# Splitting attention rows into 16-bit planes on two engines instead of one, in a top-k attention and ELU kernel

## Chip, cores and metric

The kernel runs on one core of a Trainium2 chip. The metric is the device time of one execution in microseconds (us). An engine of the core is named as the profile names it: PE is TensorE (PEld its weight loads), DVE is VectorE, ACT is ScalarE, POOL is GpSimd, SP is SyncE, which here only issues DMAs. Each engine works through its own instructions in the order in which the program lists them, and waits on semaphores for the others.

## The reference

Attention over 8 batches, 8 heads, 576 positions and 64 dimensions, in which each query keeps only its 32 highest scores; then a feed-forward layer with an ELU over all 4608 tokens.

```python
scores = q @ k.T / sqrt(64)                     # (8, 8, 576, 576)
kth    = np.partition(scores, -32)[..., -32]    # the 32nd highest of each row
scores = np.where(scores >= kth, scores, -1e9)
attn   = exp(scores - rowmax); attn /= attn.sum() + 1e-9
x      = (attn @ v), heads side by side         # (4608, 512)
h      = x @ w_in                               # (4608, 2048)
g      = np.where(h > 0, h, np.exp(np.minimum(h, 0)) - 1)
out    = g @ w_out                              # (4608, 512)
```

In the kernel the weight matrices arrive as words of 64 bits and are decoded on the chip in the first steps.

## The kernel before, in words

The attention is cut into 144 **steps**. A step is one tile of 128 queries (or the 64 left over of two heads) for two heads: a score tile `sc` of 128 partitions by 2 rows of 576 numbers (here "row 0" and "row 1": one head each). Work on one step is spread over several rounds of the main loop (lines 839 to 885). Round n does, in program order:

- the transfers and transpositions of keys, queries and values planned for this round (lines 840, 841; `load_halves` issues eight DMAs on SP, `load_v` four);
- the scores of step n+2: PE matmuls (L338), and ACT copies them to `sc` (L346);
- `attend` for a group whose transposed weights are expected (L489 on PE, L516 on ACT);
- `spread` for step n-1: a small subtraction on POOL (L379) from which the exponential of the mask takes its bias;
- `select` for step n: DVE finds the 32 highest in four passes of MAX8 and MATCH_REPLACE8 (L358, L365, L372), listed between the other things as quarters of the round;
- `mask` for step n-1, row 0 after the first quarter, row 1 after the second: two ACT passes over a row (L399, L400), the second an exponential with its sum;
- the transposition of the attention weights of step n-2, called `done`. Up to round 12 PE turns them in nine blocks of 128 by 128 (`turn`, L435) and ACT copies them out (L436). From round 13 on a path over memory is used: `split` copies a row of `sc` on ACT into two planes of 16-bit halves (L451) and SP writes the planes to a buffer in DRAM, `halves` (L452); after row 1, `cross` reads the buffer with a transposing DMA into `et` (L461);
- `normalise` for step n-1 at the end of the round: five small POOL operations (L410 to L414), then a scaling of each row (L416).

After each quarter `feed` places pieces of the feed-forward layer that are due: `hidden` (PE matmuls L564; ACT L574, L577, L579, L583), the ELU sums ("gates", POOL L534), and `project` or `product` (PE L592, L654; ACT L662; POOL L610). The pieces are chosen when the program is written, from costs and due times, so the order on each engine is fixed. `product` also streams prepared weight tiles `tw` through SP (L696).

What the order of the work around the change hangs on:

- the tile `planes` has one buffer (`late["p"]`, `bufs=1`, line 218): a second split waits until the DMA of the first has landed;
- `halves` has three buffers, `et` two, `sc` five;
- SP issues in program order: a transfer that waits for its data holds back all behind it;
- `turned` notes the round of the `cross` with the group, and the main loop calls `attend` in the second round after that (lines 847, 848).

In round n of the kernel before, row 0 of step n-2 is split at the start of the round, row 1 after the second quarter, and the transposing DMA is issued after the third. In the last two rounds the two steps left are split as well.

Of the kernel before, what the change touches and what calls it, by code (L numbers as in the profile page):

```python
# [24 lines left out]
class Tile:  # L25
# [6 lines left out]
    def __init__(self, b, qt, rows, block, cols):  # L32
        self.b, self.qt, self.rem = b, qt, qt == 4
        self.rows = rows
        self.block = block
        self.cols = cols
        self.ql = cols.stop - cols.start
# [21 lines left out]
class Step:  # L59
# [7 lines left out]
    def __init__(self, t, hp, group, at):  # L67
        self.t, self.hp = t, hp
        self.group, self.at = group, at
        self.masked = self.normal = self.turned = False  # L70
        if t.rem:
            rows = [(4 * hp, 0), (4 * hp + 2, 0), (4 * hp + 3, 1), (4 * hp + 1, 1)]
            self.heads = [
                (h, i, slice(64 * (n % 2), 64 * (n % 2) + 64))
                for n, (h, i) in enumerate(rows)
            ]
        else:
            self.heads = [(2 * hp + i, i, slice(0, 128)) for i in range(2)]
# [3 lines left out]
def kernel(  # L82
# [9 lines left out]
    nc = tc.nc  # L92
# [115 lines left out]
    def settle():  # L208

        if decode or late or blocks[0].left or any(x[3] == 0 for x in ffn):  # L210
            return
        raws.close()
        late["f"] = ctx.enter_context(tc.tile_pool(name="f", bufs=2))
        late["g"] = ctx.enter_context(tc.tile_pool(name="g", bufs=2))
        late["x"] = ctx.enter_context(tc.tile_pool(name="xt", bufs=2))
        late["e"] = ctx.enter_context(tc.tile_pool(name="e", bufs=2))
        late["t"] = ctx.enter_context(tc.tile_pool(name="t", bufs=TB))
        late["p"] = ctx.enter_context(tc.tile_pool(name="p", bufs=1))
        late["in"] = ctx.enter_context(tc.tile_pool(name="in", bufs=2))
# [100 lines left out]
    def turn_qk(whole=False):  # L320
        while turning:
            if next(turning[0], turning) is turning:
                turning.pop(0)
            elif not whole:
                return
# [25 lines left out]
    def select(u, more=False):  # L351

        u.first = small.tile([P, 2, 8], FP32, tag="m1", name="m1")
        u.last = small.tile([P, 2, 8], FP32, tag="m4", name="m4")
        cur = [u.sc[:, i, :] for i in range(2)]
        found = [u.first[:, i, :] for i in range(2)]
        for i in range(2):
            nc.vector.max(found[i], cur[i])  # L358
        if more:
            hook()  # L360
        yield
        wk = [wkpool.tile([P, S], FP32, tag=f"wk{i}", name="wk")[:] for i in range(2)]
        for r in range(TOP_K // 8 - 1):
            for i in range(2):
                nc.vector.match_replace(wk[i], found[i], cur[i], TAKEN)  # L365
            cur = wk
            for i in range(2):
                if r < TOP_K // 8 - 2:
                    found[i] = small.tile([P, 8], FP32, tag=f"m{i}", name="m")[:]
                else:  # L370
                    found[i] = u.last[:, i, :]
                nc.vector.max(found[i], cur[i])  # L372
            hook()
            yield

    def spread(u):

        u.den = small.tile([P, 8], FP32, tag="den", name="den")
        nc.gpsimd.tensor_tensor(  # L379
            u.den[:, 2:4], u.last[:, :, 7], u.first[:, :, 0], ALU.subtract  # L380
        )
# [22 lines left out]
    def normalise(u):  # L404

        if u.normal:
            return
        u.normal = True
        den, rec = u.den[:, 4:6], u.den[:, 6:8]
        nc.gpsimd.tensor_scalar_add(den, u.den[:, 0:2], EPS)  # L410
        nc.gpsimd.tensor_tensor(rec, den, power[:], ALU.pow)
        nc.gpsimd.tensor_tensor(den, den, rec, ALU.mult)
        nc.gpsimd.tensor_scalar(den, den, -1.0, 2.0, ALU.mult, ALU.add)
        nc.gpsimd.tensor_tensor(rec, rec, den, ALU.mult)  # L414
        for i in range(2):
            nc.gpsimd.tensor_scalar(  # L416
                u.sc[:, i, :], u.sc[:, i, :], rec[:, i : i + 1], 1.0, ALU.mult, ALU.mult
            )
# [23 lines left out]

    def split(u, i):

        if u.turned:
            return
        if i == 0:
            u.halves = halves.tile([P, 2, 2, S], U16, tag="h", name="halves")
        t = late["p"].tile([P, 2, S], U16, tag="p", name="planes")
        words = u.sc[:, i, :].bitcast(U16).rearrange("p (k w) -> p w k", w=2)  # L450
        nc.scalar.copy(t[:], words)  # L451
        nc.sync.dma_start(u.halves[:, :, i, :], t[:])  # L452

    def cross(u):

        if u.turned:
            return
        g = u.group
        if g.et is None:
            g.et = etpool.tile([P, 2 * J + 1, len(g.tiles), P], FP32, tag="et", name="et")  # L460
        nc.sync.dma_start_transpose(  # L461
            g.et[:, :, u.at, :].bitcast(U16),
            u.halves[:].rearrange("q w i k -> (q w) (i k)"),
        )
        turned(u)

    def turned(u):

        u.turned = True
        if u.at == len(u.group.tiles) - 1:  # L470
            closing.append((place[0] // 4, u.group))

    def attend(g):
        t = g.tiles[0]
# [47 lines left out]
    place = [0]  # L522

    def close_gates(keep=0, upto=None):

        while gates:
            put, group, dst, n, apart = gates[0]
            if put > place[0] - keep if upto is None else group > upto:  # L530
                return
            gates.pop(0)
            if apart:
                nc.gpsimd.tensor_tensor(dst, n, dst, ALU.add)  # L534
                continue
            nc.vector.scalar_tensor_tensor(
                out=dst, in0=n, scalar=-1.0, in1=dst, op0=ALU.add, op1=ALU.add
            )
# [190 lines left out]
    while ends:  # L729
        n = 1 if len(blocks) <= J or len(ends) <= J + 1 else 2  # L730
# [5 lines left out]
    for b in range(B):  # L736
        first[b] = len(steps)
        tiles = []
        for qt in range(J + 1):
# [8 lines left out]
            t = Tile(b, qt, rows, blk, slice(c0, c0 + n))  # L748
# [3 lines left out]
        for qts in orders[b]:  # L752
# [3 lines left out]
            for qt in qts:  # L756
                n = len(steps)
                tiles[qt].block.ready = n + 2.0 if n <= tight else n + 3.25
    NS = len(steps)
# [37 lines left out]
    def feed(n, share):  # L797

        place[0] += 1
        close_gates(2 if n > tight + 3 else 6)  # L800
        fed["at"] = max(fed["at"], n)
        ahead = [(w - fed["sum"]) / (x - fed["at"]) for x, w in due if x > fed["at"]]
        if ahead:
            fed["over"] += max(0.0, share * min(ahead))
        fed["at"] += share
        while ffn and decoded[0] >= ffn[0][1] and 0.5 * ffn[0][0] <= fed["over"]:
            cost, _, piece, _ = ffn.pop(0)
            fed["over"] -= cost
            fed["sum"] += cost
            piece()  # L810
            settle()
# [22 lines left out]
    def step(n):  # L834
        return steps[n] if 0 <= n < NS else None

    closing, settled = [], tight + 4
    main, rest, other = slice(0, J), slice(J, J + 1), slice(J + 1, 2 * J + 1)
    for n in range(NS + 3):
        for fn, args in todo.pop(n, []):  # L840
            fn(*args)
        ahead, cur, prev, done = step(n + 2), step(n), step(n - 1), step(n - 2)
        passes = select(cur, n < tight) if cur else iter(range(4))
        if ahead and n > 1:
            scores(ahead)
        steady = settled <= n < NS
        while steady and closing and closing[0][0] < n - 1:
            attend(closing.pop(0)[1])
        if prev and n > tight:
            spread(prev)  # L850
        crossed = n > settled
        if done and crossed:
            split(done, 0)
        next(passes)
        feed(n, 0.25)
        while closing and not steady:
            attend(closing.pop(0)[1])
        if prev:
            mask(prev, 0, n <= tight)
        if n > 1:  # L860
            turn_qk()
        next(passes)
        feed(n, 0.25)
        if done and not crossed:
            turn(done, main)
            turn(done, rest)
        elif done:
            split(done, 1)
        if prev:
            mask(prev, 1, n <= tight)  # L870
        next(passes)
        feed(n, 0.25)
        if done and not crossed:
            turn(done, other)
        elif done:
            cross(done)
        next(passes)
        if prev:
            normalise(prev)
        if spare and n >= first[1] - 2:  # L880
            difference(*spare.pop(0))
        feed(n, 0.25)
        turn_qk(True)
        if n < 2:
            scores(ahead)
# [36 lines left out]
```

## Time and profile before

| | |
|---|---|
| median of three executions | 1848.02 us (1846.99 to 1848.38) |
| the profiled execution | 1837.74 us, of which the span of the instructions is 1835.6 us |
| mean granted TensorE clock | 0.919 |
| instructions | 26765 |
| POOL busy, DMA moved | 875.2 us, 271.92 MB |

The span runs from the first to the last instruction of the program; the profile gives for each engine the time in which it executes ("busy"), and for each idle time what ended it: `A <- B` means that A waited and that B released it. The timeline lists instructions with start, duration, engine and line; neighbours of one kind are merged with their count. The chain of waits goes back from the last instruction to whatever released it, and again from there.

### The profile page before, as it was taken

The numbers are of one execution on the slowest core, as the hardware profiler recorded it, in microseconds if no ns is written. First come the engines' busy times: TensorE is split into PE (matmuls) and PEld (weight loads), VectorE is DVE, ScalarE is ACT, GpSimd is POOL, SyncE is SP. The second block draws the span as 40 slices with busy tenths as digits, with TensorE's granted clock in tenths as the row PEclk, the third lists the DMA queues.
The fourth block names the chain that finished last, engine by engine and source line by source line (L and its number), as shares of the span: only waits on it lengthen the run. The fifth ranks groups of instructions, "written<-read, shape, count | busy, mean of one in ns | idle before, by whom it ended". The sixth has DMA issues, their size and how long they took to land.

```text
span 1835.6 us, 26765 instructions
## 1 busy us (share of the span) xinstructions
PE 1496.8 (82%) x8535; PEld 1109.2 (60%) x8535; DVE 1460.6 (80%) x2976; ACT 1316.5 (72%) x2321; POOL 875.2 (48%) x1535
## 2 busy tenths in 40 slices
PE   4798878777888787987888696977888787889988
PEld 3476645545666566765666575755666565667765
DVE  6999998777888697978787399887878769788900
ACT  6977757658695767786778677785859576768861
POOL 4963335434554454545454536353544535363430
PEclk9799998888998998998999898998899889899999
DMA  7503544564748575667657665748564665564440
GB/s 231 190 24 75 132 131 133 137 161 117 213 117 215 128 194 136 175 156 167 174 156 174 154 169 125 206 110 217 124 183 128 171 159 156 156 165 116 116 112 22
DMA packets 603340, 271.92 MB, mean 148 GB/s; under 512 B 496704, under 2 KB 565824, under 8 KB 603200
## 3 DMA queue, kind: packets, MB, share of 16 engines
q1 hardware_dynamic: 602000, 269.92, 56.3%
q8 instruction: 68, 1.11, 0.3%
q14 instruction: 72, 0.59, 0.1%
q10 hardware_dynamic: 1200, 0.30, 0.1%
HBM read 99.61 MB, written 92.08 MB: 104 GB/s over the span
## 4 chain that ended last, share of the span: by engine, by line
ACT 26%; PE 22%; DMA 18%; DVE 11%; POOL 10%; SPq 7%; issue 6%; DVEq 0%; ACTq 0%; POOLq 0%
DMA halves<-planes 14%; ACT planes L451 8%; PE ops L654 8%; PE hps L564 5%; DVE wk L365 5%; ACT sc L399 4%; ACT sc L400 4%; PE ops L592 4%; DVE m L372 3%; PE avps L489 3%; DMA tw<-kept 3%; POOL sc L416 2%; SPq L238 2%; PE scps L338 2%; ACT sc L346 2%
## 5 line engine op out<-in xcount | busy, mean ns | idle before, releaser
L564 PE MATMUL hps<-xT,w_in 128*128 128x256 f32 (+1 forms) x2944 | 574.1, 354 | 96.1 <-ACT gT L577 91.7
L372 DVE MAX8 m<-wk 128x8 f32<-128x576 f32 x864 | 609.6, 745 | 7.4 <-POOL den L379 7.2
L564 PEld LDWEIGHTS hps<-xT,w_in 128*128 128x128 f32 x2944 | 487.6, 203 | 179.2 <-ACT gT L577 104.0
L451 ACT COPY planes<-sc 128x1152 uint16<-128x1152 uint16 x266 | 306.8, 1153 | 308.7 <-DMA halves<-planes 245.1
L365 DVE MATCH_REPLACE8 wk<-m,wk 128x576 f32<-128x576 f32 x576 | 422.9, 741 | 0.0
L358 DVE MAX8 m<-sc 128x8 f32<-128x576 f32 x288 | 203.3, 747 | 222.4 <-ACT sc L346 221.0
L410 POOL TENSOR_SCALAR den<-den 128x2 f32<-128x2 f32 x144 | 32.3, 225 | 719.6 <-ACT sc L400 718.5
L654 PE MATMUL ops<-tw,gT 128*128 128x256 f32 x832 | 219.2, 419 | 97.1 <-DMA tw<-kept 79.2
L654 PEld LDWEIGHTS ops<-tw,gT 128*128 128x128 f32 x832 | 167.1, 207 | 141.2 <-DMA tw<-kept 89.1
L400 ACT ACTIVATE sc<-sc,den 128x576 f32<-128x576 f32 x288 | 223.3, 775 | 36.2 <-POOL den L379 20.2
L489 PE MATMUL avps<-et,vT 128*64 128x128 f32 (+2 forms) x2400 | 199.3, 316 | 53.5 <-DMA et<-halves 48.9
L338 PE MATMUL scps<-kqT 64*128 64x288 f32 (+1 forms) x1280 | 205.5, 458 | 30.9 <-ACT kqT L314 12.6
L399 ACT ACTIVATE sc<-sc,m 128x576 f32<-128x576 f32 x288 | 223.2, 775 | 0.4 <-DVE m L372 0.4
L416 POOL TENSOR_SCALAR sc<-sc,den 128x576 f32<-128x576 f32 x288 | 213.5, 751 | 14.9
L489 PEld LDWEIGHTS avps<-et,vT 128*64 128x64 f32 x2400 | 138.8, 145 | 124.6 <-issue 52.9
L365 DVE MATCH_REPLACE8 wk<-m,sc 128x576 f32<-128x576 f32 x288 | 211.4, 741 | 0.0
L654 PE MATMUL ops<-w_out,gT 128*128 128x256 f32 x624 | 160.6, 413 | 45.2 <-POOL den L410 23.9
L534 POOL TENSOR_TENSOR gT<-n,gT 128x512 f32<-128x512 f32 x136 | 173.3, 1275 | 41.6 <-ACT n L583 41.5
L346 ACT ACTIVATE sc<-scps 128x576 f32<-128x576 f32 x288 | 169.9, 642 | 28.8 <-PE scps L338 28.6
L338 PEld LDWEIGHTS scps<-kqT 64*128 64x128 f32 (+1 forms) x1280 | 110.9, 191 | 107.7 <-issue 32.9
L654 PEld LDWEIGHTS ops<-w_out,gT 128*128 128x128 f32 x624 | 125.5, 207 | 78.8 <-POOL den L410 26.7
L592 PE MATMUL ops<-w_out,gT 128*128 128x512 f32 x320 | 145.1, 606 | 0.7 <-POOL tw L711 0.7
(57 smaller groups left out, 1257.8 us busy)
## 6 DMA issues: line engine op xcount, KB each, us to landing
halves<-planes SPq DMA_DIRECT2D x266, 288.0 KB, 2.6
tw<-kept SPq DMA_DIRECT2D x208, 256.0 KB, 3.8
raw<-in_moe_w_in_dram SPq DMA_DIRECT2D x16, 512.0 KB, 5.0
vT<-in_v_dram SPq DMA_DIRECT2D x64, 128.0 KB, 2.7
raw<-in_moe_w_out_dram SPq DMA_DIRECT2D x16, 512.0 KB, 3.8
out_dram<-osb SPq DMA_DIRECT2D x32, 256.0 KB, 4.3
kin<-in_k_dram SPq DMA_DIRECT2D x112, 72.0 KB, 2.8
qin<-in_q_dram SPq DMA_DIRECT2D x112, 72.0 KB, 2.7
```

Of the source, the lines that this page charges most:

```text
L338: nc.tensor.matmul(wide[i][rows, half, 0:HS], kq[part, q0 : q0 + u.t.ql], kq[part, k0 : k0 + HS], start=True, stop=True,)
L346: nc.scalar.activation(u.sc[:, i, :].rearrange("p (a s) -> p a s", a=2), wide[i][:, :, 0:HS], AF.Copy, scale=scale,)
L365: nc.vector.match_replace(wk[i], found[i], cur[i], TAKEN)
L372: nc.vector.max(found[i], cur[i])
L399: nc.scalar.activation(sc, sc, AF.Prelu, scale=-1.0, bias=low, alpha=1.0 / STEEP)
L400: nc.scalar.activation(sc, sc, AF.Exp, scale=-STEEP, bias=gap, accum_out=u.den[:, i : i + 1])
L416: nc.gpsimd.tensor_scalar(u.sc[:, i, :], u.sc[:, i, :], rec[:, i : i + 1], 1.0, ALU.mult, ALU.mult)
L451: nc.scalar.copy(t[:], words)
L489: nc.tensor.matmul(ps[i * D : (i + 1) * D, cols], vt[:, 2 * J + i if c == J else i * J + c, :], w, start=(c == 0), stop=(c == J),)
L564: nc.tensor.matmul(blk.h[:, f % bank, :], w_in[:, i, f * P : (f + 1) * P], blk.xT[:, i, 0:n_tok], start=(i == 0), stop=(i == NC - 1),)
L592: nc.tensor.matmul(blk.o[:], blk.gT[f // NG][:, f % NG, s * P : (s + 1) * P], w_out[:, f, :], start=(f == 0), stop=(f == NF - 1),)
L654: nc.tensor.matmul(sums, x[:, f, :], w, start=opens and f == 0, stop=f == NG - 1, skip_group_check=not opens,)
```

## The change

A step's row 1 is split on POOL, at the end of the round in which the step was normalised (round n-1 for step n-2), with the same shapes and the same `planes` buffer. Its write to DRAM is kept as a function and issued in the next round after the second quarter. Row 0 is split on ACT as before, but after the third quarter, half a round later than before. The transposing DMA is moved from after the third quarter of round n to after the first quarter of round n+1 (`past` is step n-3 seen from there), and the number noted for its group is reduced by one, so that `attend` comes in the same round as before. The last two steps (rounds 144 and 145) go back to `turn` on PE.

```diff
     def split(u, i):
 
-        if u.turned:
-            return
-        if i == 0:
+        if u.halves is None:
             u.halves = halves.tile([P, 2, 2, S], U16, tag="h", name="halves")
         t = late["p"].tile([P, 2, S], U16, tag="p", name="planes")
         words = u.sc[:, i, :].bitcast(U16).rearrange("p (k w) -> p w k", w=2)
-        nc.scalar.copy(t[:], words)
-        nc.sync.dma_start(u.halves[:, :, i, :], t[:])
+        if i == 0:
+            nc.scalar.copy(t[:], words)
+        else:
+            nc.gpsimd.tensor_copy(t[:], words)
+        return lambda: nc.sync.dma_start(u.halves[:, :, i, :], t[:])
...
         if u.at == len(u.group.tiles) - 1:
-            closing.append((place[0] // 4, u.group))
+            closing.append((place[0] // 4 - (u.halves is not None), u.group))
...
-        crossed = n > settled
-        if done and crossed:
-            split(done, 0)
+        crossed = settled < n < NS
+        past = step(n - 3)
         next(passes)
+        if past and past.halves is not None:
+            cross(past)
         feed(n, 0.25)
...
         elif done:
-            split(done, 1)
+            done.write()
         if prev:
             mask(prev, 1, n <= tight)
         next(passes)
...
         elif done:
-            cross(done)
+            split(done, 0)()
         next(passes)
         if prev:
             normalise(prev)
+            if settled <= n < NS - 1:
+                prev.write = split(prev, 1)
```

`Step` gets two new fields, `halves` and `write`, both empty at first.

More of the change, by code (lines that the diff above doesn't have):

```diff
@@ L70, in __init__ @@
         self.masked = self.normal = self.turned = False
+        self.halves = self.write = None
         if t.rem:
@@ L450, in split @@
         words = u.sc[:, i, :].bitcast(U16).rearrange("p (k w) -> p w k", w=2)
-        nc.scalar.copy(t[:], words)
-        nc.sync.dma_start(u.halves[:, :, i, :], t[:])
+        if i == 0:
[3 more added lines that the diff above has]
+        return lambda: nc.sync.dma_start(u.halves[:, :, i, :], t[:])
     def cross(u):
-        if u.turned:
-            return
         g = u.group
```

## Prediction

> **What bounds the kernel now.** I read the busy times and the chain of waits on the page first, then the waits of ACT, then two steps of the timeline.
>
> ```profile
> span 1835.6 us, 26765 instructions
> ...
> PE 1496.8 (82%) x8535; PEld 1109.2 (60%) x8535; DVE 1460.6 (80%) x2976; ACT 1316.5 (72%) x2321; POOL 875.2 (48%) x1535
> ...
> DMA halves<-planes 14%; ACT planes L451 8%; PE ops L654 8%; PE hps L564 5%; DVE wk L365 5%; ACT sc L399 4%; ACT sc L400 4%; PE ops L592 4%; DVE m L372 3%; PE avps L489 3%; DMA tw<-kept 3%; POOL sc L416 2%; SPq L238 2%; PE scps L338 2%; ACT sc L346 2%
> ```
>
> By busy time PE and DVE lead. But 22% of the chain are the ACT copies into the planes and the writes of the planes. The waits say why:
>
> ```profile
> ACT planes L451 <- DMA halves<-planes: 245.1, 93, 8.0
> ACT planes L451 <- POOL sc L416: 62.4, 45, 2.7
> ACT e L662 <- PE ops L654: 41.1, 23, 5.7
> ACT sc L346 <- PE scps L338: 28.6, 24, 2.4
> ACT osb L662 <- PE ops L654: 25.9, 16, 2.5
> ...
> ACT xT L516 <- PE avps L489: 21.1, 13, 3.8
> ACT sc L400 <- POOL den L379: 20.2, 20, 2.4
> ACT n L574 <- PE hps L564: 13.2, 8, 3.0
> ...
> DVE m L358 <- ACT sc L346: 221.0, 79, 11.9
> PE avps L489 <- DMA et<-halves: 48.9, 29, 4.0
> ```
>
> ACT is busy for 1316.5 us and waits 307.5 us before the splits and some 150 us in the other rows shown: nearly the whole span is spoken for. ACT has no slack, while DVE waits for ACT (221 us). So ACT's order, with what it waits for, sets the pace.
>
> ```profile
> 1000.04 1.15 ACT L451 COPY planes<-sc 128x1152 uint16<-128x1152 uint16 x1 [2.95 <-DMA halves<-planes]
> 1001.10 0.77 ACT L399 ACTIVATE sc<-sc,m 128x576 f32<-128x576 f32 x1
> ...
> 1001.90 0.77 ACT L400 ACTIVATE sc<-sc,den 128x576 f32<-128x576 f32 x1
> 1002.59 0.19 ACT L400 ACTIVATION_READ_ACCUMULATOR sc<-sc,den 128x1 f32 x1
> 1002.68 0.57 ACT L574 ACTIVATE n<-hps 128x512 f32<-128x512 f32 x1
> ...
> 1003.79 3.68 PE L564 MATMUL hps<-xT,w_in 128*128 128x256 f32 x8 [3.98 <-ACT gT L577]
> 1003.80 2.12 SPq L461 DMA_TRANSPOSE et<-halves  x1
> ...
> 1004.29 0.63 ACT L583 ACTIVATE n<-n 128x512 f32<-128x512 f32 x1
> ...
> 1005.88 1.15 ACT L451 COPY planes<-sc 128x1152 uint16<-128x1152 uint16 x1
> 1006.02 2.28 SPq L238 DMA_DIRECT2D kin<-in_k_dram  x4
> ...
> 1008.40 2.17 SPq L238 DMA_DIRECT2D qin<-in_q_dram  x4
> ...
> 1010.66 4.62 SPq L452 DMA_DIRECT2D halves<-planes  x2
> ...
> 1011.03 5.45 PE L564 MATMUL hps<-xT,w_in 128*128 128x256 f32 x24
> ...
> 1013.56 1.15 ACT L451 COPY planes<-sc 128x1152 uint16<-128x1152 uint16 x1 [2.74 <-DMA halves<-planes]
> ```
>
> The split at 1005.88 ends at 1007.0, but SP is busy with eight key and query loads until 1010.6; only then does it issue the write, and the next split waits for the landing, until 1013.56. From the start of a split to the landing of its write are 3.76 us where SP is free (1000.04 to 1003.80, where the transposing DMA, which waits for it, is issued).
>
> ```profile
> L451 ACT COPY planes<-sc x266: 1134/1152/1184, 163.8 to 1783.9; 128x1152 uint16<-128x1152 uint16 x133
> L452 SPq DMA_DIRECT2D halves<-planes x266: 533/553/1033, 171.6 to 1785.1; - x133
> DMA to landing us min/median/max: 2.5/2.6/5.9
> ```
>
> These 266 splits are 133 rounds in 1621 us (163.8 to 1785.0): 12.2 us a round. The change touches this stretch and the end. The busy times in it (160 to 1780), of its last part with granted clock, DMA share and GB/s at the end of the row, and summed over six parts:
>
> ```profile
> 1560.00:1780.00 220.00, 202.49 (x1399) 154.85 (x1400) 151.47 (x311) 170.27 (x298) 100.59 (x189) 0.95 0.50 134
> sum 1620.00, PE 1326.64 PEld 989.96 DVE 1314.63 ACT 1175.09 POOL 768.68; mean PE 221.11 PEld 164.99 DVE 219.10 ACT 195.85 POOL 128.11
> ```
>
> ACT is busy 8.9 us a round here, PE 10.0, DVE 9.9.
>
> **Part by part.** *ACT loses* 133 copies of 1.152 us, 153 us, and the waits before them, 307.5 us. The copy that stays waits for other things, and the wait before the exponential grows, as follows.
>
> *POOL gains* 133 copies of 128x1152 16-bit numbers, a kind that the trace does not show there. The nearest rows:
>
> ```profile
> L416 POOL TENSOR_SCALAR sc<-sc,den 128x576 f32<-128x576 f32 x288 | 213.5, 751 | 14.9
> L534 POOL TENSOR_TENSOR gT<-n,gT 128x512 f32<-128x512 f32 x136 | 173.3, 1275 | 41.6 <-ACT n L583 41.5
> L610 POOL TENSOR_TENSOR gT<-gT 128x1024 f32<-128x1024 f32 x52 | 122.9, 2363 | 1.5
> L379 POOL TENSOR_TENSOR den<-m,m 128x2 f32<-128x2 f32 x136 | 26.6, 196 | 2.5 <-DVE m L372 2.4
> ```
>
> One input, 576 elements: 0.75 us, so 1.5 us for twice as many. Two halves read as one word would give 0.75, the two-input pace (2.13 ns an element from L534 to L610, 0.18 us fixed) 2.6. I take 1.5, the row with one input, and keep 0.75 (then PE decides, first rival) and 2.6. POOL's load, 875 + 200 us, is no bound.
>
> [...]
>
> *The new wait.* The POOL copy shares the single planes buffer, so it waits for the landing of row 0's write. Behind it on POOL stand the gates (L534), for which `product` on PE waits, and the next `spread` (L379), for which ACT's exponential waits. That closes a loop, from one ACT split to the next:
>
> - split and landing of its write: 3.76
> - POOL copy 1.5, half a gate a round (136 in 133 rounds, half the places) 0.65, `spread` 0.2
> - row 0's exponential, 1001.90 to 1002.78: 0.88; row 1's two passes, 1001.10 to 1002.78: 1.68
> - feed-forward ACT work at two of four places: half of 1002.68 to 1004.92, 1.15
> - six hand-overs at some 0.08 (the exponential ended at 1002.78, the next group starts POOL that late: an estimate): 0.5
>
> Together 10.3 us a round, against ACT's own work of 8.9 - 1.15 = 7.7 a round.
>
> *SP.* The transposing DMA now comes first, then row 1's write, on which the next ACT split waits:
>
> ```profile
> L461 SPq DMA_TRANSPOSE et<-halves x133: 2115/2536/4354, 178.2 to 1787.7; - x133
> ...
> DMA to landing us min/median/max: 4.3/4.7/7.9
> ```
>
> 3.76 until row 0's write has landed, 2.5 to issue the transposing DMA, 2.6 for row 1's write: 8.9, inside 10.3. Where the eight loads stand ahead, they start after 1.15 + 0.55 and take 4.45: 6.15 + 2.5 + 2.6 = 11.3, a microsecond over. There are 28 such rounds (four for each batch after the first): 28 us. Value loads (half as many) and streamed tiles fit the 1.4 us of slack. The `sc` buffers cost nothing: the copy that frees a tile now later still stands before the copy that refills it on ACT.
>
> The weights for `attend` are issued a quarter round later relative to it (their last split moves from the half to the third quarter): 2.8 us less cover. Today's 29 waits of PE would grow by up to 81 us together; I count nothing, because PE has 293 us idle in the stretch, and keep 81 for the range.
>
> *PE's waits that reach ACT* (L662 twice, L346, L516, L574: 130 us) stay in kind. Part falls into ACT's new idle time; I keep three quarters, 97 us. That share is an estimate.
>
> *The end.* Turning the last two steps on PE shortens the way from the last exponential to `et`. It brings little, because PE is already filled there:
>
> ```profile
> 1782.36 1.31 PE L489 MATMUL avps<-et,vT 128*64 128x128 f32 x20 [1.64 <-ACT n L579]
> ...
> 1792.20 1.31 PE L489 MATMUL avps<-et,vT 128*64 128x128 f32 x20 [1.32 <-DMA et<-halves]
> ```
>
> At most 3 us of idle time can go, and 18 transpositions come, at most 4 us at the pace of the 24 matmuls above (0.23 us each). I count 0.
>
> *Sum.* 133 x 10.3 + 28 + 97 = 1499 us instead of 1621: 122 less. The profiled execution took 1837.74, 2.1 over its span; less 122 it is 1716. The median shown is 0.56% above the profiled one: **1725 us**.
>
> **Rivals.**
>
> *PE becomes the bound, all else hides.*
>
> The last part already runs with PE at 92% and a clock of 0.95. At that density the 1326.64 us of PE would fill 1442: 178 less, **1669**. For it: eight matmuls after an idle 3.98 us took 3.68 us, twenty-four in a run 5.45, so a denser PE is also a faster one, 0.23 us each instead of 0.46. Against it: the loop above leaves no room for all of PE's waits.
>
> [...]
>
> *The wait only moves to POOL.* With the copy at 2.6 us the loop is 11.4; the load rounds and three quarters of PE's 130 us then hide in it: 133 x 11.4 + 33 = 1549, 72 less, **1775**.
>
> *Slower: POOL's copy holds the round.* By the same sum the break-even is a copy of 3.1 us (133 x (8.8 + 3.1) + 33 = 1616). At 3.5, which no row excludes for halves read in steps, the stretch takes 1669, 48 more: **1896**. Every tenth of a microsecond beyond 3.1 costs 13 us. Against it: both paces that POOL shows lie below. A copy in the wrong place would show the same way.
>
> **How the numbers follow.** Chances: forecast 0.50, PE-bound 0.18, moved wait 0.19, slower 0.13. The range goes from the PE-bound case (1660) to the moved wait with part of the 81 us (1815); outside stay the slower case and some of the fast end, 0.2. Below and above 0.2%, about what a measurement of this kernel tells from no change: faster 0.84 (the first three cases, less 0.03 of the moved wait), same 0.03, slower 0.13.
>
> **What would show it.** Right: L451 133 copies; POOL's copy near 1.5 us and waiting for a DMA of the planes; ACT's wait before the planes far below 245 us; the row "sc L400 <- POOL" up from 20 us to over 100, with L379 or the copy as releaser; DVE's 221 us shrinking; rounds near 11.3 us. Wrong: a copy above 2.6 us; a write behind the transposing DMA landing after 4 us or more, which would use up the slack of 1.4; or PE's 49 us for `et` several times as long.

## The result, and the profile after

The changed kernel takes 1871.3 us (median of four) against 1848.2 for the kernel before: a ratio of 1.0124, 95% interval 1.010 to 1.0148. It is 1.2% slower, a small difference, but the interval leaves out 1, where 1725 us, 6.7% less, were forecast. The kernel before took 1835 to 1848 us on the chips used below, so experiments are given as ratios to it on the same chip.

The page of the changed kernel, with span, busy times and the chain of waits by engine and by line (the numbers of the lines moved by one: L451 is now ACT's split, L453 POOL's, L454 the write of the planes, L401 the exponential, L380 `spread`):

```profile
span 1867.3 us, 27043 instructions
...
PE 1508.0 (81%) x8553; PEld 1116.2 (60%) x8553; DVE 1461.4 (78%) x2976; ACT 1179.9 (63%) x2192; POOL 1028.3 (55%) x1666
...
PE 29%; DMA 22%; ACT 15%; DVE 13%; POOL 8%; SPq 8%; issue 5%; POOLq 0%; ACTq 0%; DVEq 0%
DMA halves<-planes 14%; PE ops L654 9%; PE hps L564 8%; PE avps L489 6%; DVE wk L366 6%; DMA et<-halves 5%; DVE m L373 4%; SPq L461 4%; ACT planes L451 3%; PE scps L339 3%; PE ops L592 3%; ACT sc L401 3%; POOL planes L453 2%; DMA tw<-kept 2%; ACT sc L400 2%
```

ACT lost 137 us of work and the span grew by 32. The writes of the planes still hold 14% of the chain, and two links stand here that the rows of before do not have: the transposing DMA's landing (5%) and SP's time to issue it (4%). The waits, longest first, with total, times and longest (the first row is POOL waiting for the exponential that `normalise` needs):

```profile
POOL den L411 <- ACT sc L401: 286.8, 117, 10.6
POOL planes L453 <- DMA halves<-planes: 262.3, 88, 8.2
DVE m L359 <- ACT sc L347: 217.2, 68, 11.8
ACT planes L451 <- DMA halves<-planes: 215.8, 68, 9.2
ACT sc L401 <- POOL den L380: 156.1, 82, 7.1
PE avps L489 <- DMA et<-halves: 152.0, 41, 9.0
...
POOL planes L453 <- ACT sc L347: 106.8, 31, 9.5
...
ACT osb L662 <- PE ops L654: 91.7, 25, 8.4
...
ACT e L662 <- PE ops L654: 71.5, 26, 5.6
...
ACT xT L516 <- PE avps L489: 32.9, 20, 6.6
ACT n L574 <- PE hps L564: 29.0, 20, 3.0
...
ACT sc L347 <- PE scps L339: 18.6, 17, 2.4
```

Set against the rows of before, ACT's account reads: busy 1316.5 to 1179.9 (137 less), before the planes 307.5 to 215.8 (92 less), for POOL's `spread` 20.2 to 156.1 (136 more), for PE in the five rows shown 130 to 244 (114 more). That is 21 more, most of the 32. What ACT gained came back as waits. Busy time and waits fill the span on every engine, so this account tells where ACT's time went, not what caused it.

The mean granted TensorE clock is 0.898 here and was 0.919 before. PE was busy 11 us longer, with 18 matmuls more: even if all of it lay on the chain, it would be a third of the 32 us. The run of the engine alone, below, is faster than the kernel before at a clock of 0.908. So the clock is not the main cause.

One round shows where. The timeline of the changed kernel, rows of SP, POOL, PE and ACT:

```profile
308.16 0.54 SPq L454 DMA_DIRECT2D halves<-planes  x1
...
310.84 1.14 POOL L453 COPY planes<-sc 128x1152 uint16<-128x1152 uint16 x1 [3.14 <-ACT sc L347]
...
311.95 1.27 POOL L711 TENSOR_TENSOR tw<-w_out 128x512 f32<-128x512 f32 x1
...
313.25 0.34 SPq L714 DMA_DIRECT2D kept<-tw  x1
...
313.69 3.25 SPq L461 DMA_TRANSPOSE et<-halves  x1
...
316.99 4.53 SPq L454 DMA_DIRECT2D halves<-planes  x2
...
319.00 2.40 PE L489 MATMUL avps<-et,vT 128*64 128x256 f32 x10 [5.34 <-DMA et<-halves]
...
319.81 1.15 ACT L451 COPY planes<-sc 128x1152 uint16<-128x1152 uint16 x1 [3.96 <-DMA halves<-planes]
```

Row 0's planes are written at 308.16 and POOL splits the next row 1 from 310.84 to 311.98. (The view names an ACT copy as what released POOL at 310.84; the write of row 0 landed at 310.69, just before.) But SP first has the store of a prepared weight tile (L714), whose data POOL computes only after the split (L711), and stands still for it from 308.70 to 313.25; then the transposing DMA, which it takes 3.25 us to issue; and only at 316.99 row 1's planes, ready for five microseconds. ACT waits for their landing until 319.81, PE for `et` until 319.00. Both wait for SP.

For the 130 rounds from one ACT split to the next I took the starts and landings from the trace (means in us; the transposing DMA is that of the round, the write that of the row 1 after it). "Queue" is the time in which SP stands before other things, or has not come to it:

```
                                forecast  changed  all at once  loads later
split, to landing of its write    3.8       3.9        4.6          4.4
queue ahead of transposing DMA    0.2       1.3        0.1          0.5
issuing the transposing DMA       2.5       2.7        2.5          2.5
queue ahead of row 1's write      -         0.6        0.1          0.6
landing of row 1's write          2.6       3.2        2.9          3.1
landing to ACT's next split       -         0.8        1.7          1.0
split to split                   10.3      12.5       11.8         12.1
```

In the mean the way to the last landing takes 11.7 us in the changed kernel, where the forecast had 9.1, and 10.3 for the round before PE's share. In 72 of the 130 rounds ACT's next split starts within 0.15 us of that landing: there the chain over SP sets the round. In the 68 rounds without another DMA between row 0's write and the transposing DMA the round has a median of 11.0 us, in the 21 with just the eight key and query loads 12.5 (mean 13.9), in the 8 with a stored weight tile 12.8.

### The profile page after: what moved, and what is told of

It is laid out like the page before. It is cut to its first block, busy times and chain, and to the rows that moved or that the text cites. A ratio compares the mean times of both kernels' runs of the same rounds, so it can differ in the third digit from the quotient of the medians.

```text
span 1867.3 us, 27043 instructions
## 1 busy us (share of the span) xinstructions
PE 1508.0 (81%) x8553; PEld 1116.2 (60%) x8553; DVE 1461.4 (78%) x2976; ACT 1179.9 (63%) x2192; POOL 1028.3 (55%) x1666
## 4 chain that ended last, share of the span: by engine, by line
PE 29%; DMA 22%; ACT 15%; DVE 13%; POOL 8%; SPq 8%; issue 5%; POOLq 0%; ACTq 0%; DVEq 0%
DMA halves<-planes 14%; PE ops L654 9%; PE hps L564 8%; PE avps L489 6%; DVE wk L366 6%; DMA et<-halves 5%; DVE m L373 4%; SPq L461 4%; ACT planes L451 3%; PE scps L339 3%; PE ops L592 3%; ACT sc L401 3%; POOL planes L453 2%; DMA tw<-kept 2%; ACT sc L400 2%
## 5 line engine op out<-in xcount | busy, mean ns | idle before, releaser
L373 DVE MAX8 m<-wk 128x8 f32<-128x576 f32 x864 | 625.6, 777 | 39.7 <-POOL den L380 39.5
L564 PE MATMUL hps<-xT,w_in 128*128 128x256 f32 (+1 forms) x2944 | 562.7, 350 | 53.0 <-ACT gT L577 53.0
L564 PEld LDWEIGHTS hps<-xT,w_in 128*128 128x128 f32 x2944 | 480.3, 200 | 133.9 <-ACT gT L577 61.2
L366 DVE MATCH_REPLACE8 wk<-m,wk 128x576 f32<-128x576 f32 x576 | 431.6, 772 | 0.0
L453 POOL COPY planes<-sc 128x1152 uint16<-128x1152 uint16 x131 | 149.9, 1144 | 382.9 <-DMA halves<-planes 262.3
L489 PE MATMUL avps<-et,vT 128*64 128x128 f32 (+2 forms) x2400 | 230.1, 349 | 154.9 <-DMA et<-halves 152.0
L401 ACT ACTIVATE sc<-sc,den 128x576 f32<-128x576 f32 x288 | 223.8, 777 | 166.2 <-POOL den L380 156.1
L489 PEld LDWEIGHTS avps<-et,vT 128*64 128x64 f32 x2400 | 156.6, 162 | 239.0 <-issue 113.7
L451 ACT COPY planes<-sc 128x1152 uint16<-128x1152 uint16 x131 | 150.3, 1147 | 217.5 <-DMA halves<-planes 215.8
L654 PE MATMUL ops<-w_out,gT 128*128 128x256 f32 x624 | 151.9, 396 | 43.9 <-POOL gT L534 39.6
L654 PEld LDWEIGHTS ops<-w_out,gT 128*128 128x128 f32 x624 | 118.6, 195 | 73.3 <-POOL gT L534 45.6
```

The lines of the kernel that those rows point to most:

```text
L401: nc.scalar.activation(sc, sc, AF.Exp, scale=-STEEP, bias=gap, accum_out=u.den[:, i : i + 1])
L453: nc.gpsimd.tensor_copy(t[:], words)
L489: nc.tensor.matmul(ps[i * D : (i + 1) * D, cols], vt[:, 2 * J + i if c == J else i * J + c, :], w, start=(c == 0), stop=(c == J),)
L564: nc.tensor.matmul(blk.h[:, f % bank, :], w_in[:, i, f * P : (f + 1) * P], blk.xT[:, i, 0:n_tok], start=(i == 0), stop=(i == NC - 1),)
L654: nc.tensor.matmul(sums, x[:, f, :], w, start=opens and f == 0, stop=f == NG - 1, skip_group_check=not opens,)
```

## The experiments

Theory S: SP's order closes the round. Theory E: `et` comes late for `attend`, and PE's wait passes on to ACT. Theory B: the single planes buffer, whatever SP does.

**The changed kernel again.** Unaltered, on the chip of three of the runs below.

> The changed kernel unaltered, on the chip of the runs beside it, as their measure. Its ratio to the kernel before should be 1.01 to 1.015 again, ACT's wait before its planes 200 to 230 us and PE's wait for et 140 to 165. In its first profile every MAX8 and MATCH_REPLACE8 of VectorE was 30 ns longer than in the kernel before; if GpSimd's 16-bit copies caused it, it shows again, else the means are back at 745 and 741 ns.

Ratio 1.0151 (1.011 to 1.0193); 213.8 us before ACT's planes, 150.7 us for `et`. MAX8 (L373) takes 746 ns here and took 777 in the first profile: the longer DVE instructions there have nothing to do with POOL's copies and are no part of the cause.

**The end alone.** In the kernel before:

```diff
-        crossed = n > settled
+        crossed = settled < n < NS
```

> The kernel before with one part of the change alone: the last two steps are turned by TensorE. My prediction costs it at nothing, because PE is filled at the end: within 3 us of the kernel before. If the end counts, up to 9 us faster (the way from the last exponential to et is 16 us over memory and some 7 us over PE).

Ratio 0.9999 (0.998 to 1.0018). The end costs and brings nothing, as forecast.

**The engine alone.** In the kernel before, row 1's split in its old place, on POOL:

```diff
-        nc.scalar.copy(t[:], words)
+        if i == 0:
+            nc.scalar.copy(t[:], words)
+        else:
+            nc.gpsimd.tensor_copy(t[:], words)
```

> The kernel before with the engine alone changed: row 1 is split on POOL instead of ACT, in its old place after the second quarter; order on SP and places of all else as before. If taking 153 us of copies off ACT is what counts, ratio 0.93 to 0.97. Theory S: the write of row 0 still stands behind the round's loads on SP, POOL's copy waits for its landing and the exponential for POOL: ACT's waits before the planes fall from 307 us to 50 to 150, those for POOL rise from 20 to over 100, ratio 0.97 to 1.00.

Ratio 0.987 (0.984 to 0.990). The waits of this kernel (L454 is POOL's split, L452 ACT's):

```profile
POOL planes L454 <- DMA halves<-planes: 459.8, 95, 12.1
...
ACT sc L346 <- POOL planes L454: 139.4, 57, 7.4
ACT planes L452 <- POOL sc L416: 126.7, 75, 4.6
...
ACT planes L452 <- DMA halves<-planes: 17.2, 6, 4.1
```

POOL instead of ACT waits for the landing, and ACT for POOL: for the score buffer which the late copy holds, and for the normalised row. (I had expected the wait at the exponential; it stayed at 29.5 us.) Still 1.3% faster: the engine is no loss. So it is the moves that make the changed kernel slower than the kernel before.

**The transposing DMA at once.** In the changed kernel, with `cross(past)` removed and the number for `attend` set back:

```diff
             split(done, 0)()
+            cross(done)
```

> The changed kernel with the transposing DMA issued right behind the write of row 0, in the same round, so that the next round's loads stand behind it and not ahead of it. Theory S (SP's order closes the round: split on ACT, landing, whatever stands ahead on SP, transposing DMA, write of row 1, landing, next split on ACT): the loads move from one side of the transposing DMA to the other, the chain to the next split keeps its length; ACT's wait before its planes stays at 215 +- 40 us, time 1850 to 1880. Theory E (the lost cover of attend: PE's wait for et, 152 us instead of 49, passes on to ACT): PE's wait for et falls below 60 us, ACT's waits for PE by about 100, time 1780 to 1820.

Ratio 1.0231 (1.020 to 1.026).

```profile
ACT planes L451 <- DMA halves<-planes: 238.7, 75, 10.4
...
PE avps L489 <- DMA et<-halves: 78.2, 41, 5.2
```

PE's wait for `et` halves, and the time does not fall: 1877 us, inside the range of S. As theory S says, what stood ahead of the transposing DMA now stands behind it, ahead of row 1's write (2.3 us there on average). E alone does not explain the result.

**Row 1's write first.** In the changed kernel `done.write()` is called just ahead of `cross(past)`:

```diff
         next(passes)
+        if done and crossed:
+            done.write()
         if past and past.halves is not None:
             cross(past)
...
-        elif done:
-            done.write()
```

> The changed kernel with the write of row 1 issued at the start of the round, ahead of the transposing DMA of the step before. Theory S: the 2.7 us in which SP issues the transposing DMA leave the chain to the next split; ACT's wait before its planes falls from 216 us below 80, time 1770 to 1820. Theory E: the transposing DMA comes 0.6 us later still, PE's wait for et stays at 150 to 180 us, time 1860 to 1885.

Ratio 1.0045 (1.0026 to 1.0063).

```profile
PE avps L489 <- DMA et<-halves: 192.2, 59, 8.1
...
ACT xT L516 <- PE avps L489: 102.5, 48, 5.0
...
ACT planes L451 <- DMA halves<-planes: 55.1, 29, 5.8
```

ACT's wait before the planes falls as S says, from 216 to 55 us, but only 1% of the time comes with it, 1844 us, between the ranges of S and E: now `et` is late, and ACT waits 102.5 us for `attend`.

**Row 1's write at once.** The same further on: the write is issued at the end of the round before, ahead of the loads, and the transposing DMA stays.

```diff
-        elif done:
-            done.write()
...
-                prev.write = split(prev, 1)
+                split(prev, 1)()
```

> The changed kernel with one of the two moves of the all-at-once kernel: the write of row 1 is issued as soon as POOL has split it, at the end of the round and ahead of the next round's loads; the transposing DMA stays in the next round. Theory S (the chain over SP alone sets the pace): ACT's wait before its planes below 60 us and nearly the whole gain of the all-at-once kernel, ratio to before 0.965 to 0.98. Theory S+E (with the chain shortened, the late et is next): PE waits 150 to 220 us for et, ratio 0.985 to 1.005.

Ratio 1.0519 (1.0485 to 1.0553), far slower than either theory had it.

```profile
PE avps L489 <- DMA et<-halves: 267.9, 57, 13.5
...
ACT xT L516 <- PE avps L489: 186.6, 58, 10.7
...
ACT planes L451 <- DMA halves<-planes: 4.2, 7, 1.0
```

The transposing DMA now stands behind that write, for which SP waits until POOL has split, and behind the loads: 3.8 us after its data has landed on average. ACT's wait before its planes is gone (4.2 us), as S had it, and yet this is the slowest kernel of all: that wait alone does not measure the loss.

**Both at once.** The two edits above together: nothing is held back, and both transfers stand ahead of the next round's loads.

> The changed kernel with nothing held back: the write of row 1 is issued as soon as POOL has split it, at the end of the round, and the transposing DMA right behind the write of row 0, so that both stand ahead of the next round's loads. Theory S: nothing but the three transfers is left in the chain, about 9.5 us, ACT's wait before its planes falls below 100 us and the round to 11.3 us or less; time 1740 to 1800. Theory E: the same early et, no more: 1780 to 1820 with ACT's wait before its planes unchanged. Theory B (the single planes buffer itself, whatever SP does): the landing of each write is still waited for by the other engine, both waits for the planes stay above 150 us, time 1840 to 1880.

Ratio 0.9701 (0.968 to 0.972).

```profile
POOL planes L453 <- DMA halves<-planes: 261.9, 88, 8.8
...
ACT sc L401 <- POOL den L380: 208.8, 93, 7.5
PE avps L489 <- DMA et<-halves: 113.7, 45, 6.7
...
ACT osb L662 <- PE ops L654: 104.4, 27, 10.2
ACT e L662 <- PE ops L654: 97.1, 30, 9.1
...
ACT planes L451 <- DMA halves<-planes: 35.7, 36, 2.6
...
ACT xT L516 <- PE avps L489: 27.1, 15, 6.2
```

Only issues on SP were moved against the changed kernel, so its order there costs 4.4% (1.0151 to 0.9701). The wait before ACT's planes is nearly gone, and the landing is 1.7 us ahead of the next split in the mean. The time is the one that S gave, the round is not (11.8 us, not 11.3 or less), and one of the two waits that theory B named stays: POOL's copy waits 261.9 us for a landing, and ACT 208.8 us behind POOL. Against the run with the late transposing DMA only the place of that DMA differs: 8%, with 113.7 us of waiting for `et` on PE in place of 267.9 and 27.1 for `attend` on ACT in place of 186.6. On another chip the same kernel gave:

> The all-at-once kernel once more, beside the one with two planes buffers on the same chip: ratio to before 0.968 to 0.973.

0.971 (0.969 to 0.973).

**The loads later.** The changed kernel with only the loads moved on SP, behind row 1's write:

```diff
-        for fn, args in todo.pop(n, []):
-            fn(*args)
+        planned = todo.pop(n, [])
+        later = [x for x in planned if n > settled and x[0] in (load_halves, load_v)]
+        for fn, args in planned:
+            if (fn, args) not in later:
+                fn(*args)
...
             done.write()
+        for fn, args in later:
+            fn(*args)
```

> The changed kernel with one thing moved: from round 13 on the planned loads of keys, queries and values are issued after the write of row 1 (after the second quarter) and not at the start of the round, so that they stand behind the transposing DMA and the write. Theory S: the rounds with loads (a median of 12.5 us and a mean of 13.9 from split to split where eight loads stand ahead, against 11.0 and 11.4 where nothing does) come down to the others, some 45 rounds by 1 to 2.5 us: ratio to before 0.96 to 0.99 instead of 1.0151, ACT's wait before its planes below 160 us. If the loads only happen to stand in rounds that are long anyway: ratio 1.005 to 1.02, the wait at 200 us or more.

Ratio 0.9954 (0.993 to 0.998), just above the range of S, with the wait at 155.6 us, just inside it. The order of the planes' own transfers was not touched, so the place of the loads on SP alone is worth 2%: more than the whole loss.

**Two planes buffers.** They need 2.3 KB a partition more; to make room, the streamed weight tiles went from six buffers to four; the all-at-once kernel with four is the measure.

```diff
-    TF, TB = 2, 6
+    TF, TB = 2, 4
...
-        late["p"] = ctx.enter_context(tc.tile_pool(name="p", bufs=1))
+        late["p"] = ctx.enter_context(tc.tile_pool(name="p", bufs=2))
```

> The all-at-once kernel with four buffers for streamed weight tiles instead of six: the measure for the kernel with two planes buffers, which needs their room. Ratio to before 0.97 to 0.985; PE's wait for tw, 68 us, may double.

With the first edit alone: 0.9876 (0.985 to 0.991); ACT's waits for PE's products rise to 260 us.

> The all-at-once kernel with two planes buffers (and four streamed tiles instead of six, to make room). POOL's copy need not wait for the landing of row 0's write any more, nor ACT's for row 1's. If these waits are what is left of the chain (POOL's copy waits 262 us, ACT's exponential 209 us behind it), ACT's wait for POOL falls below 60 us and the time by 4 to 6% against the all-at-once kernel with four streamed tiles: ratio to before 0.92 to 0.94. If PE is next (ACT's waits for PE's products, 201 us, and PE's for et and tw), the waits only change their name: less than 2% against it, ratio 0.96 to 0.98.

With both: 0.9467 (0.942 to 0.951), just outside the 0.92 to 0.94 that I gave, 4.1% below the kernel with four streamed tiles, and the fastest of all: 1740 us beside 1835.

```profile
ACT osb L662 <- PE ops L654: 129.0, 27, 12.1
...
ACT e L662 <- PE ops L654: 119.5, 27, 10.5
...
ACT xT L516 <- PE avps L489: 82.0, 37, 6.2
ACT sc L401 <- POOL den L380: 63.3, 50, 3.6
...
POOL planes L453 <- DMA halves<-planes: 13.0, 6, 5.2
```

POOL's wait for a landing falls from 291.6 us to 13.0, ACT's wait behind POOL's copy from 192 to 63. So theory B holds for what is left once SP's order is mended; in the changed kernel itself, with SP as it is, it was not tried.

**`attend` a quarter round later**, in the all-at-once kernel: the call moves from the start of the round to just after the first `feed`.

> The all-at-once kernel with attend a quarter round later on PE (after the first feed instead of before it). Theory E (the late et is what is left): PE's wait for et falls from 114 us below 70, ratio to before 0.95 to 0.965 instead of 0.970. If PE only waits there for what it would wait for anyway: 0.965 to 0.975.

Ratio 0.9684 (0.965 to 0.972): PE's wait for `et` falls to 39.3 us, ACT's for `attend` rises from 27.1 to 74.8, and the time stays. The wait only moved from PE to ACT; whether an earlier `et` would help there was not tried.

## Why the prediction was wrong, point by point

- *ACT has no slack and sets the pace.* Only in part. That ACT's busy time and waits fill the span does not show it, and taking the copies off ACT with all else in place (the engine alone) brought 1.3%. By the chain ACT's own work came first before, and comes behind PE and the DMAs in the changed kernel (15%, against 29 and 22%). Before:

```profile
ACT 26%; PE 22%; DMA 18%; DVE 11%; POOL 10%; SPq 7%; issue 6%; DVEq 0%; ACTq 0%; POOLq 0%
```

- *POOL's copy takes 1.5 us.* It takes less:

```profile
L453 POOL COPY planes<-sc x131: 1143/1144/1147, 164.2 to 1789.7; 128x1152 uint16<-128x1152 uint16 x131
```

With that the moved wait at 2.6 us and the slow copy above 3.1 us are out; the sign came from somewhere else. A number takes 0.99 ns (1144 ns for 1152), where L416, the row behind my 1.5, takes 1.30 an element (751 ns for 576).
- *The new wait on POOL.* Right in kind: 20 to 156 us at the exponential, 209 where SP is in order.
- *SP: 28 us for the load rounds, all else in the slack.* **This is the step that failed.** The chain of 8.9 us leads to the next split only if SP turns to each transfer when its data is there. It does not: eight loads, stored tiles, streamed tiles and the transposing DMA stand ahead, each can wait for another engine itself (L714 for POOL, 74.2 us in 16 waits; L696 for PE, 44.6 us in 50), and the delays add up to 1.3 and 0.6 us in the mean round where I had 0.2. Row 1's write took 3.2 us to land in the mean, where I had put in the median of 2.6 (the mean before was 2.8 already). I overlooked the 16 stores of L714 altogether. So the chain took 11.7 us, not 9.1, and overran the loop of 10.3 in which it was to hide. Loads moved: 2% back. Both transfers ahead of the loads: 4.4% back.
- *A quarter round less cover for `attend`: counted at nothing.* Also wrong. PE's wait for `et` went from 49 to 152 us, 41 waits in place of 29; I had kept 81 us for the range, and the growth was 103. PE's idle time was no sure cover: with the write at once, where PE waits 268 us, ACT waits 187 us for `attend`, and with only the transposing DMA issued earlier the time is 8% lower. What the 152 us cost in the changed kernel itself is not shown: with half of them gone, and the delay moved to row 1's write, its time did not fall.
- *Three quarters of PE's 130 us reach ACT: 97.* Measured 244 in the same five rows, and 274 in the all-at-once kernel. Why they grew is not shown. The length of the round alone does not tell: they stand at 232 with the engine alone (1817 us) and at 217 with the transposing DMA at once (1877 us).
- *The sum.* 133 x 10.3 + 28 + 97 is 1495, not 1499, which changes nothing. Of the way from the forecast's ratio of 0.934 to the measured 1.012 to 1.015, SP's order is the 4.4% from 0.970 up. What lies between 0.934 and 0.970 stays open: in the all-at-once kernel the round is 11.8 us, where the prediction had 11.3, and both the loop over the single planes buffer and PE's waits are still in it. The second buffer takes 4.1% off although the waits for PE rise to 397 us.
- *The end: nothing.* Right.
- *Rivals.* PE as the bound did not come: PE stayed at 81% busy. The slower case was given 0.13 for another mechanism. My list of signs named the right places (the 49 us "several times as long", the slack of the write behind the transposing DMA used up), but the sum did not carry them, and the reason given for the second was not the one: the write landed after 3.2 us in the mean, not 4 or more, but was issued late.

## What to carry to other kernels

Where one queue issues in order, write out what stands ahead of a moved transfer in each kind of round, and what each of these waits for; here it paid to issue the two transfers that feed each other's buffers as soon as their data was there, ahead of the bulk loads, and neither move alone brought more than 1%. A deferred issue is not free because its data is needed late: here holding back two issues turned a gain of 3% into a loss of 1.2%. An engine's idle time is cover only if no engine that counts waits for that engine: with the write at once PE waited 268 us for `et`, and ACT 187 us for PE.

## What the runs showed of the hardware

In the changed kernel SP was occupied 2.3 to 4.4 us by issuing one transposing DMA, against 0.55 (median) for a plain write of half the data, and nothing behind it in its queue started before it was done (the next DMA on SP began at least 0.04 us after its end, in all 131 cases). POOL split 1152 16-bit numbers a partition in 1.144 us, as fast as ACT (1.152). In three profiles (the first of the changed kernel, the loads later, `attend` a quarter round later) the MAX8 on `wk` took 774 to 803 ns on average, in all others 745 to 750, also with POOL's copies in the kernel; why stays open.
